# A transformer block on one Trainium2 core: attention in visits of one token tile and four units, and the first FFN layer of chunk 0 by token tiles

## The chip, the core and the metric

The kernel runs on one core of a Trainium2 chip. The core has five engines that run their own instruction queues in order and meet at semaphores: TensorE (PE: matmuls, and with them the loads of the stationary operand, PEld), VectorE (DVE), ScalarE (ACT), GpSimd (POOL) and SyncE (SP, which here issues the DMAs). The metric is the device time of one launch in microseconds (us); lower is better.

## The reference

One pre-norm transformer block over a sequence of 2048 tokens with 576 features, in bf16. The attention has 32 heads of 18 features and works in four segments of 512 tokens: inside a segment it is causal softmax attention, and what lies in earlier segments enters through a compressed memory. The FFN has 4608 hidden features.

```python
# per segment s, per head; phi(t) = t+1 where t>0, exp(t) elsewhere; g = sigmoid(beta)
a_dot = softmax(qs @ ks.T / sqrt(18) + causal_mask) @ vs
a_mem = (phi(qs) @ M) / (phi(qs) @ z + 1e-6)
o     = g * a_mem + (1 - g) * a_dot
M, z  = M + phi(ks).T @ vs, z + phi(ks).sum(tokens)
# the block
h   = x + concat(o) @ wo          # q, k, v come from layernorm(x) @ wq, wk, wv
out = h + gelu_tanh(layernorm(h) @ w1 + b1) @ w2 + b2
```

## The kernel before

The 2048 tokens are cut into eight chunks of 256, a chunk into two token tiles of 128. A segment is two chunks, an even and an odd one. Seven generators ("streams") each produce the work of one stage for all chunks in turn:

- `stream_P(tl)`, one for each token tile of a chunk: load x, layernorm (DVE, with a power on POOL), transpose, the projections to q, k and v (four groups of five matmuls of 432 columns, L294 and L295), transposes of q and k into `QT` and `KT`, and phi of k for the memory. For the first two chunks transposes are matmuls (L320, L401), later they are DMA transposes.
- `stream_M`: the memory `MZacc` and its gated form `MZ_blk`.
- `stream_A`: the attention. A *unit* is four heads (one group g), one tile of 128 queries and one tile of 128 keys. A *visit* is up to 512 score columns for each of the four heads: the scores (L482) are four matmuls at a time, one in each 32-row group of the array, into the four banks `st`; ACT takes the exponential of all of it into one of three buffers `pt` (L488); POOL zeroes what lies above the diagonal (L492), one instruction for each unit on the diagonal; PE multiplies with v (L507), accumulating in the bank `ox`. `st` is there once, so the next visit's scores wait for the exponential. Before the change a visit is one group g with both query tiles: key tiles 0 and 1 together, then 2 and 3 in an odd chunk. Since units above the diagonal are left out, a visit holds 3 units (384 columns) or 4 (512 columns). There are 8 visits in an even chunk and 16 in an odd one, 96 in all; 320 units. After two groups `finish` divides by the softmax's sum and adds the memory's part (L547 to L563). Attention of chunk c begins when P is done for both its token tiles.
- `stream_B(tl)`: the output projection with `wo`, the residual, the second layernorm and its transposition into `xn2T`. It begins when the attention of the whole chunk is done.
- `stream_F1`: the first FFN layer, 36 tiles of 128 hidden features, each five matmuls of 256 columns (L294, L295), evicted two tiles at a time by DVE (L703); then GELU on ACT in pieces of 18 tiles (L711). w1 is streamed from memory; for chunk 0 there are five buffers of four tiles each. It begins when both halves of B are done.
- `stream_F2`: the second FFN layer, four accumulations of 36 matmuls of 288 columns for each chunk (L737).

Every engine's order is fixed while the program is built. The streams hand operations to a planner (`op`, `begin`, `step`): each operation carries an engine, an assumed duration, what it reads and writes, and a due time (now plus an entry of the table `SLACK`). The planner steps through an assumed time; an engine that is free takes the ready operation that is due first, and PE takes the first stream in a list of preferences that can go on. Sorted by the planned start, the operations are then issued. Where PE has nothing to do before the first FFN matmul, the planner puts in *filler* matmuls on the tile `pq` that compute nothing used (L775). ACT has to load a table when it changes between exponential and GELU.

The instructions thus stand in a planned order, but the chip waits on real semaphores: an engine whose next instruction isn't ready stands still, whatever lies behind it.

Of the kernel before, what the change touches and what calls it, by code (L numbers as in the profile page):

```python
# [16 lines left out]
def kernel(  # L17
# [40 lines left out]
    def sbuf(name, shape, dt=BF16):  # L58
# [10 lines left out]
    SLACK = dict(lnp=5, lnb=6.5, pow=4, apply=-8, ek_k=4, relu_k=9, min_k=0.5, add_k=10, mz=2.5, exp=-5, ek=9.5,  # L69
                 relu=13.5, min=4.5, add=0, hb=27, gelu=17.5, finish=3.5, mem=-2, sum=-2, out=8, hd=17, xp=0.5, xb=10,  # L70
                 t_x=34, t_q=19.5, t_k=34, t_o=23, t_h=14, w1=1.5, w2=16, hc=25.5, evict=0, qk=-3, ot=-7, mask=0,
                 lead=1.5, balance=21)
    ops = []
    now, dma_free, table = 0.0, 0.0, "exp"
    free_at = {"PE": 0.0, "SP": 0.0, "ACT": 0.0, "DVE": 0.0, "POOL": 0.0}
    queue = {e: [] for e in free_at}
    writer, readers = {}, {}

    class Op:
        start, end, n = None, NEVER, None  # L80
# [132 lines left out]
    bank_slots.free.append("ox")  # L213
    f_slots = bank_slots
# [82 lines left out]
    def layernorm(who, src, skey, dst, dkey, f32, slack):  # L297
# [6 lines left out]
        def first():  # L304
# [10 lines left out]
                                           op0=ALU.subtract, op1=ALU.mult), ["st" + who, skey], [dkey], slack=slack + SLACK["apply"])  # L315
# [11 lines left out]
    half_P, half_B, t_phi, gelued, begun_P = set(), set(), set(), set(), set()  # L327
# [12 lines left out]
    def stream_P(tl):  # L340
        who = f"p{tl}"
        for c in range(NCH):
# [78 lines left out]
            op("DVE", 0.25, lambda: nc.vector.tensor_scalar(out=ek[:], in0=ek[:], scalar1=1.0, scalar2=None, op0=ALU.min), (), ["ek"], slack=SLACK["min_k"])  # L421
# [403 lines left out]
```

## Time and profile before

| | |
|---|---|
| three runs | 501.04, 501.07 and 501.58 us; median 501.07 us |
| profiled execution | 498.7 us, of which its span (first to last instruction) is 497.0 us |
| granted TensorE clock, mean | 0.996 |
| busy in the span | PE 480.1, PEld 363.1, ACT 292.2, DVE 283.8, POOL 206.6 us |
| PE instructions | 5525 matmuls |

How to read it: a matmul's record is longer than the distance to the next one, since matmuls overlap in the array. The price of a matmul in a stream is therefore taken from the distance of starts, not from its recorded duration. In rows of the trace by time the columns are: start, us from the first start to the last end, engine, line, operation, operands, shape, count, and in brackets the idle time before it with what ended it.

### The profile page before, as it was taken

Reading aid. Unit: us, or ns where it says so; the run is one execution under the profiler, and the core shown is the slowest. Engines: PE = TensorE matmul, PEld = TensorE weight load, DVE = VectorE, ACT = ScalarE, POOL = GpSimd, SP = SyncE. Lnnn points to the kernel's source line nnn. Section 1 sums busy time; section 2 is a strip of 40 time slices with the busy share of each in tenths; the row PEclk is TensorE's granted clock in tenths of the full one; section 3 lists DMA queues with packets and bytes.
Section 4 is the critical chain, followed back from the end, with each engine's and each line's share of the span. In section 5 each row is a group of like instructions: output and inputs, shape, how many; then the busy total and the mean of one; then the engine's idle time right before and its main releaser. Section 6 shows DMA issues by size and latency. Waiting matters only on the chain.

```text
span 497.0 us, 13329 instructions
## 1 busy us (share of the span) xinstructions
PE 480.1 (97%) x5525; PEld 363.1 (73%) x5525; DVE 283.8 (57%) x696; ACT 292.2 (59%) x221; POOL 206.6 (42%) x291
## 2 busy tenths in 40 slices
PE   8999899798999999999999999999999999999997
PEld 5756578556577877766587787767887878878885
DVE  5868765487577534699456434876734443634411
ACT  3477868953557878657518687666357867122210
POOL 5565541279556331779331423596404242200000
PEclk9999999899999999999999999999999999999999
DMA  8985575549877453958977345777854445765411
GB/s 245 299 281 161 102 164 156 137 58 187 175 169 194 143 169 99 228 106 173 196 199 194 124 153 155 175 113 239 195 172 126 144 138 154 203 206 155 139 37 47
DMA packets 117340, 80.89 MB, mean 163 GB/s; under 512 B 56392, under 2 KB 115232, under 8 KB 117280
## 3 DMA queue, kind: packets, MB, share of 16 engines
q1 hardware_dynamic: 117248, 80.04, 62.3%
q8 instruction: 43, 0.70, 0.6%
q14 instruction: 17, 0.14, 0.1%
q0 software_dynamic: 32, 0.01, 0.1%
HBM read 60.10 MB, written 7.08 MB: 135 GB/s over the span
## 4 chain that ended last, share of the span: by engine, by line
PE 81%; DVE 7%; DMA 6%; ACT 2%; SPq 1%; issue 1%; POOL 0%; DVEq 0%; ACTq 0%
PE bank L294 34%; PE bank L737 23%; PE bank L295 8%; PE ox L507 6%; PE st L482 5%; PE ox L737 2%; DMA w1g<-in_B_w_dram 2%; DMA wqkv<-in_A_wk_dram 1%; DMA xT<-xn 1%; PE ox L294 1%; DVE xn L314 1%; DMA xT<-o_nat 1%; ACT hT L711 1%; DVE stats_p L301 1%; DVE r L550 1%
## 5 line engine op out<-in xcount | busy, mean ns | idle before, releaser
L488 ACT ACTIVATE pt<-st 128x2048 bf16<-128x2048 f32 (+1 forms) x96 | 153.0, 1594 | 99.8 <-PE st L482 98.6
L703 DVE CAST hT<-bank 128x512 bf16<-128x512 f32 x139 | 95.7, 689 | 104.3 <-PE bank L295 103.3
L737 PE MATMUL bank<-w_sb,hT 128*128 128x288 bf16 x1044 | 150.7, 287 | 3.0 <-ACT hT L711 3.0
L294 PE MATMUL bank<-xn2T,w1g 128*128 128x256 bf16 x1032 | 149.1, 272 | 0.4 <-DMA w1g<-in_B_w_dram 0.4
L737 PEld LDWEIGHTS <-hT 128*128 128x128 bf16 x1152 | 109.3, 98 | 31.8 <-ACT hT L711 3.3
L492 POOL TENSOR_SCALAR_AFFINE_SELECT pt<-pt 128x512 bf16<-128x512 bf16 x128 | 80.3, 652 | 97.7 <-ACT pt L488 97.6
L294 PEld LDWEIGHTS <-w1g 128*128 128x128 bf16 x1072 | 99.8, 97 | 20.4 <-issue 5.1
L711 ACT ACTIVATE hT<-hT 128x4608 bf16<-128x4608 bf16 (+1 forms) x22 | 65.9, 2996 | 46.0 <-DVE hT L703 45.9
L295 PE MATMUL bank<-xn2T,w1g 65*128 65x256 bf16 x258 | 70.7, 274 | 0.8 <-DMA w1g<-in_B_w_dram 0.8
L294 PE MATMUL bank<-wqkv,xT 128*128 128x432 bf16 x252 | 56.4, 345 | 2.8 <-DMA xT<-xn 2.6
L294 PEld LDWEIGHTS <-xT 128*128 128x128 bf16 x384 | 34.8, 98 | 27.2 <-DMA xT<-xn 3.0
L507 PEld LDWEIGHTS <-pt 128*128 128x128 bf16 x1280 | 43.9, 96 | 9.6 <-issue 6.0
L507 PE MATMUL ox<-v_aug,pt 128*128 128x19 bf16 x1280 | 47.0, 172 | 0.7 <-DVE o_nat L557 0.3
L523 POOL TENSOR_TENSOR pq<-ek,pq 128x512 bf16<-128x512 bf16 x24 | 27.9, 1163 | 27.2 <-DVE ek L522 27.0
L482 PE MATMUL st<-QT,KT 32*128 32x256 bf16 (+1 forms) x768 | 34.8, 255 | 0.7 <-ACT pt L488 0.6
L563 POOL TENSOR_TENSOR o_nat<-t,t 128x288 bf16<-128x288 f32 x24 | 19.4, 806 | 31.2 <-DVE t L560 31.1
L295 PEld LDWEIGHTS <-w1g 65*128 65x128 bf16 x268 | 26.1, 97 | 4.5 <-DMA w1g<-in_B_w_dram 1.4
L741 DVE TENSOR_TENSOR ot<-bank,hc 128x288 bf16<-128x288 f32 x29 | 13.2, 456 | 24.9 <-PE bank L737 21.3
L482 PEld LDWEIGHTS <-KT 32*128 32x128 bf16 x768 | 11.7, 92 | 18.9 <-issue 17.4
L376 ACT CAST qk_pad<-bank 128x432 bf16<-128x432 f32 x31 | 16.0, 520 | 14.4 <-PE bank L295 14.1
L645 POOL TENSOR_TENSOR h_t<-h_t,b_bc 128x576 f32<-128x576 f32 x16 | 20.5, 1279 | 7.1 <-DVE xn L314 7.1
L294 PE MATMUL bank<-wo_t,xT 128*128 128x288 bf16 x128 | 21.3, 293 | 1.9 <-DMA xT<-o_nat 0.9
(98 smaller groups left out, 476.6 us busy)
## 6 DMA issues: line engine op xcount, KB each, us to landing
w1g<-in_B_w_dram SPq DMA_DIRECT2D x67, 512.0 KB
w_sb<-in_B_w_dram SPq DMA_DIRECT2D x6, 864.0 KB
hd<-h_t SPq DMA_DIRECT2D x16, 288.0 KB
hc<-hd SPq DMA_DIRECT2D x32, 144.0 KB
w1g<-in_B_w_dram SPq DMA_DIRECT2D x67, 64.0 KB
x_b<-in_A_x_dram SPq DMA_DIRECT2D x18, 144.0 KB
hT<-in_B_w_dram SPq DMA_DIRECT2D x5, 512.0 KB
out_dram<-ot SPq DMA_DIRECT2D x16, 144.0 KB
```

What stands on the lines that cost most here:

```text
L294: nc.tensor.matmul(out=out_ap, lhsT=lhsT_of(slice(0, P), k), rhs=rhs_of(slice(0, P), k), start=(k == 0), stop=False)
L295: nc.tensor.matmul(out=out_ap, lhsT=lhsT_of(slice(0, KTAIL), 4), rhs=rhs_of(slice(0, KTAIL), 4), start=False, stop=True)
L482: nc.tensor.matmul(out=st4[:, i, o:o + (2 - lo) * P], lhsT=KTs[(s0 + kt // 2) % 3][rows, g, (kt % 2) * P:(kt % 2 + 1) * P], rhs=QTs[c % 2] ...
L488: op("ACT", 0.18 + 4 * off * 0.00083, lambda: nc.scalar.activation(out=pt[:, :, 0:off], in_=st4[:, :, 0:off], func=ACT.Exp, scale=scale), ...
L492: op("POOL", 0.675, lambda o=o: nc.gpsimd.affine_select(out=pt[:, :, o:o + P], in_=pt[:, :, o:o + P], pattern=[[0, 4], [1, P]], compare_op ...
L507: nc.tensor.matmul(out=oxv[:, g % 2, qt, i, :], lhsT=pts[slot][:, i, blk:blk + P], rhs=v_augs[(2 * s0 + kt) % 6][:, 4 * g + i, :], start=o ...
L523: op("POOL", 1.15, lambda: nc.gpsimd.tensor_tensor(out=pq[:], in0=e_g, in1=pq[:], op=ALU.add), ["ek"], ["pq"], slack=SLACK["add"])
L563: op("POOL", 0.7, lambda: nc.gpsimd.tensor_tensor(out=o_dst, in0=t1v, in1=t2v, op=ALU.add), ["t1", "t2"], ok, slack=SLACK["sum"])
L645: op("POOL", 1.36, lambda: nc.gpsimd.tensor_tensor(out=h_t[:], in0=h_t[:], in1=b2_bc[:], op=ALU.add), ["b2"], [("h", tl)], slack=SLACK["hb"])
L703: op("DVE", 0.684, lambda hT=hT, jp=jp, acc=acc: nc.vector.tensor_copy(out=hT[:, 2 * jp:2 * jp + 2, :], in_=acc), [b], [("hT", c % 2, jp)] ...
L711: op("ACT", (f1 - f0) * Q * 0.00083 + 0.18, lambda hT=hT, f0=f0, f1=f1: nc.scalar.activation(out=hT[:, f0:f1, :], in_=hT[:, f0:f1, :], fun ...
L737: nc.tensor.matmul(out=acc, lhsT=hT[:, q, tl * P:(tl + 1) * P], rhs=w2_sb[:, q, hs], start=(q == 0), stop=(q == NF - 1))
```

## The change

Five things change.

1. **Visits.** A visit is now four units of one token tile qt of the queries: `units` runs over four groups (sixteen heads, one half gh of the heads) and the key tiles that the query tile sees, and is cut into pieces of four. All 80 visits have 512 columns. A score matmul has 128 columns, so a visit is sixteen matmuls in four rounds of four row groups (before: eight matmuls in two rounds). `finish` and the memory's part work on one token tile and sixteen heads, as often as before (32 and 24 times).
2. **Finer dependences.** Attention of a token tile begins when P of that tile is done, and B of a tile begins when the attention of that tile is done. With more than two masked units in a visit, the products with v wait for the masks two units at a time.
3. **F1 of chunk 0.** The first 20 of the 36 hidden tiles (five w1 buffers, `AHEAD` = 5) are done for token tile 0 as soon as B of that tile is done, and later again for token tile 1, in matmuls of 128 columns. The other 16 tiles are done for both together, as before. The first GELU piece of chunk 0 then has 22 tiles and the second 14 (before 18 and 18).
4. **The planner** now also assumes that certain DVE operations and POOL's wait for each other (`port`).
5. **All entries of `SLACK`** are new numbers, so the order moves everywhere.

```diff
-    SLACK = dict(lnp=5, lnb=6.5, pow=4, apply=-8, ek_k=4, relu_k=9, min_k=0.5, add_k=10, mz=2.5, exp=-5, ek=9.5,
+    SLACK = dict(head=0, lnp=5.5, lnb=9.5, pow=-8.5, apply=8, ek_k=23, relu_k=40, min_k=5, add_k=9, mz=5, exp=13.5,
...
+        if getattr(o, "port", False):
+            dur += max(0.0, port_until["POOL" if o.eng == "DVE" else "DVE"] - now)
+            port_until[o.eng] = now + dur
...
-    def scores(c, g, pieces, slot):
+    def scores(c, qt, units, slot):
...
+            for n, (g, kt) in enumerate(units):
                 for i in range(4):
                     rows = slice(32 * i, 32 * i + 32)
+                    nc.tensor.matmul(out=st4[:, i, n * P:(n + 1) * P],
+                                     lhsT=KTs[(c - c % 2 + kt // 2) % 3][rows, g, (kt % 2) * P:(kt % 2 + 1) * P],
+                                     rhs=QTs[c % 2][rows, g, qt * P:(qt + 1) * P], start=True, stop=True, tile_position=(32 * i, 0))
...
+            for qt in range(2):
+                for gh in range(2):
+                    units = [(g, kt) for g in range(4 * gh, 4 * gh + 4) for kt in range(2 * (c % 2) + qt + 1)]
+                    visits += [(c, qt, gh, n == 0, n + 4 == len(units), units[n:n + 4]) for n in range(0, len(units), 4)]
...
+                yield need(lambda: (c, qt) in half_P and (c < 2 or (c - 2, qt) in half_B) and (seg == 0 or 2 * seg - 1 in done_M),
...
+                parts = [(0, 1), (2, 3)] if sum(kt == own for _, kt in units) > 2 else [(0, 1, 2, 3)]
...
-            yield need(lambda: c in done_A, xT_slots, idle=False)
+            yield need(lambda: (c, tl) in half_A, xT_slots, idle=False)
...
-            for jp in range(NF // 2):
+            if c == 0:
+                for tl in range(2):
+                    for n in range(AHEAD):
...
+                        yield need(lambda: (0, tl) in half_B, f_slots, xk[tl:tl + 1] + wk)
...
+                            op("PE", 5 * 0.0565, lambda acc=acc, a=a, wt=wt, tl=tl: mm5(
+                                acc[:, a, :], lambda r, k: wt[r, k, a * P:(a + 1) * P],
+                                lambda r, k: xn2T[0][r, k, tl * P:(tl + 1) * P]), xk[tl:tl + 1] + wk, [b])
...
+            for jp in range(0 if c else 2 * AHEAD, NF // 2):
```

What this does to the queues is seen at three places. The first is PE at the first FFN matmul of the program. `xn2T_88` is the transposed input of the FFN for chunk 0, `w1g_66` the first w1 buffer, `xT_87` the input of a q, k, v projection, `KT_104` the keys of chunk 0, `pt_109` a buffer of exponentials. Before, this place comes after 109 filler matmuls and 16 visits:

```order
L294 MATMUL bank_142<-wqkv,xT_87 128x432
...
L295 MATMUL bank_142<-wqkv,xT_87 128x432
L294 LDWEIGHTS w1g_66
L294 MATMUL bank_141<-xn2T_88,w1g_66 128x256
...
L295 MATMUL bank_141<-xn2T_88,w1g_66 128x256
L482 LDWEIGHTS KT_104
L482 MATMUL st_139<-QT_103,KT_104 128x256
```

After the change it comes after 70 filler matmuls and 10 visits, behind the memory's matmuls (`phik_pad`):

```order
L447 LDWEIGHTS phik_pad_95
L447 MATMUL bank_143<-v_aug_99,phik_pad_95 128x76
L300 LDWEIGHTS w1g_66
L300 MATMUL bank_141<-xn2T_88,w1g_66 128x128
...
L301 MATMUL bank_141<-xn2T_88,w1g_66 128x128
L518 LDWEIGHTS pt_109
L518 MATMUL ox<-v_aug_98,pt_109 128x19
```

The first FFN layer has moved ahead of six visits, in halves of 128 columns. Of the fillers 38 stood ahead of the first projection and 71 behind it; now 42 stand ahead and 28 behind.

The second place is ACT at the first GELU of the program (`hT_122` is the hidden layer of chunk 0, `ek` the exponential of queries for the memory). Before:

```order
L488 ACTIVATE pt_107<-st_139 128x4x384
L711 ACT_TABLE_LOAD
L711 ACTIVATE hT_122<-hT_122 128x4608
L488 ACT_TABLE_LOAD
L488 ACTIVATE pt_108<-st_139 128x2048
L488 ACTIVATE pt_109<-st_139 128x4x384
L711 ACT_TABLE_LOAD
L711 ACTIVATE hT_122<-hT_122 128x4608
```

After:

```order
L495 ACTIVATE pt_108<-st_139 128x2048
L528 ACTIVATE ek<-QT_102 128x512
L741 ACT_TABLE_LOAD
L741 ACTIVATE hT_122<-hT_122 128x5632
L495 ACT_TABLE_LOAD
L495 ACTIVATE pt_109<-st_139 128x2048
L741 ACT_TABLE_LOAD
L741 ACTIVATE hT_122<-hT_122 128x3584
```

The first piece has grown from 18 hidden tiles to 22 (5632 elements), and one exponential instead of two stands between the pieces.

The third place is PE where the second FFN layer begins (`w_sb,hT_122`). Before, sixteen of its matmuls stand in a row, then a product with v and a visit, and then the matmuls on tiles 16 to 19:

```order
L295 MATMUL bank_143<-xn2T_88,hT_123 128x256
L737 LDWEIGHTS hT_122
L737 MATMUL bank_141<-w_sb,hT_122 128x288
...
L507 LDWEIGHTS pt_109
L507 MATMUL ox<-v_aug_98,pt_109 128x19
...
L482 LDWEIGHTS KT_106
L482 MATMUL st_139<-QT_102,KT_106 128x256
```

After, sixteen stand in a row, then the output projection of chunk 1 (`wo_t`) and a visit:

```order
L301 MATMUL bank_141<-xn2T_88,hT_123 128x256
L767 LDWEIGHTS hT_122
L767 MATMUL bank_143<-w_sb,hT_122 128x288
...
L300 LDWEIGHTS xT_87
L300 MATMUL bank_142<-wo_t,xT_87 128x288
...
L489 LDWEIGHTS KT_106
L489 MATMUL st_139<-QT_102,KT_106 128x128
```

Ahead of it now stand all of the sixteen hidden tiles of chunk 0 that are done for both token tiles, with a single visit among them; behind it, tiles 16 to 19 follow after ten `wo` matmuls and one visit, and tiles 20 to 23 after a product with v, a memory product and five projection matmuls.

More of the change, by code (lines that the diff above doesn't have):

```diff
@@ L495, in scores @@
-        return placed
-    def weighted(c, g, placed, slot):
+        op("PE", 0.43, go, score_keys(c, qt, units), sk)
+        op("ACT", 1.88, lambda: nc.scalar.activation(out=pt[:], in_=st4[:], func=ACT.Exp, scale=scale), sk,
+           [("pt", slot, n) for n in range(4)], slack=SLACK["exp"], table="exp")
+        for n, (g, kt) in enumerate(units):
+            if kt == own:
+                op("POOL", 0.65, lambda n=n: nc.gpsimd.affine_select(
+                    out=pt[:, :, n * P:(n + 1) * P], in_=pt[:, :, n * P:(n + 1) * P], pattern=[[0, 4], [1, P]],
+                    compare_op=ALU.is_ge, fill=0.0, base=0, channel_multiplier=-1), (), [("pt", slot, n)], slack=SLACK["mask"])
@@ L501, in go @@
         def go():
-            opens = g % 2 == 0 and placed[0][0] == 0
-            for kt, lo, o in placed:
+            opens = first
+            for n in part:
+                g, kt = units[n]
                 for i in range(4):
-                    for qt in range(lo, 2):
-                        blk = o + (qt - lo) * P
-                        nc.tensor.matmul(out=oxv[:, g % 2, qt, i, :], lhsT=pts[slot][:, i, blk:blk + P],
-                                         rhs=v_augs[(2 * s0 + kt) % 6][:, 4 * g + i, :], start=opens, stop=False,
-                                         skip_group_check=True)
-                        opens = False
@@ L512, in weighted @@
-        n = sum(4 * (2 - lo) for _, lo, _ in placed)
-        op("PE", n * 0.025, go, [("pt", slot)] + vk, ["ox"])
-    def memory_in(c, g):
-        q2 = QTs[c % 2][:, g:g + 2, :]
-        qk = [("QT", c % 2, 0), ("QT", c % 2, 1)]
-        e_g = ek[:].rearrange("p h d -> p (h d)")[:, 0:2 * Q].rearrange("p (u q) -> p u q", u=2)
-        op("ACT", 0.63, lambda: nc.scalar.activation(out=e_g, in_=q2, func=ACT.Exp), qk, ["ek"], slack=SLACK["ek"], table="exp")
-        op("POOL", 0.61, lambda: nc.gpsimd.tensor_scalar(out=pq[:], in0=q2, scalar1=BIG, scalar2=0.0, op0=ALU.min, op1=ALU.max),
+                    nc.tensor.matmul(out=oxv[:, 4 * (g % 4) + i, :], lhsT=pts[slot][:, i, n * P:(n + 1) * P],
+                                     rhs=v_augs[(2 * s0 + kt) % 6][:, 4 * g + i, :], start=opens, stop=False, skip_group_check=True)
@@ new lines, in go, with memory_in @@
+                    opens = False
+        op("PE", len(part) * 0.1, go, [("pt", slot, n) for n in part] + value_keys(c, units), ["ox"])
+    def memory_in(c, qt, gh):
+        q4 = QTs[c % 2][:, 4 * gh:4 * gh + 4, qt * P:(qt + 1) * P]
+        qk = [("QT", c % 2, qt)]
+        e_g = ek[:].rearrange("p h d -> p (h d)")[:, 0:4 * P].rearrange("p (g q) -> p g q", g=4)
+        op("ACT", 0.63, lambda: nc.scalar.activation(out=e_g, in_=q4, func=ACT.Exp), qk, ["ek"], slack=SLACK["ek"], table="exp")
+        op("POOL", 0.62, lambda: nc.gpsimd.tensor_scalar(out=pq[:], in0=q4, scalar1=BIG, scalar2=0.0, op0=ALU.min, op1=ALU.max),
```

203 lines of the change are left out of this document (103 added, 100 removed).

## The prediction

> **What bounds the kernel now.** I read the page's busy times first, then the chain that ended last, then the busy times either side of the first FFN matmul (at 63.75 us), then who made PE wait behind it.
>
> ```profile
> span 497.0 us, 13329 instructions
> PE 480.1 (97%) x5525; PEld 363.1 (73%) x5525; DVE 283.8 (57%) x696; ACT 292.2 (59%) x221; POOL 206.6 (42%) x291
> PE 81%; DVE 7%; DMA 6%; ACT 2%; SPq 1%; issue 1%; POOL 0%; DVEq 0%; ACTq 0%
> 0.00:63.75 63.75, 58.16 (x709) 38.59 (x710) 45.23 (x130) 40.07 (x44) 36.65 (x62) 1.00 0.77 219
> 63.75:497.00 433.25, 421.99 (x4817) 324.56 (x4815) 238.60 (x567) 252.09 (x178) 169.95 (x230) 0.99 0.61 155
> PE bank L737 <- ACT hT L711: 3.0, 1, 3.0
> PE bank L294 <- DMA xT<-xn: 2.6, 1, 2.6
> PE bank L294 <- DMA xT<-o_nat: 0.9, 1, 0.9
> ```
>
> PE is the bound: 97% busy, 81% of the chain, and behind 63.75 us it stands still for 11 of 433 us. Two waits make half of that: one of 3.0 us for a GELU, one of 2.6 us for a DMA transpose. So only two things shorten the kernel: less PE work, and less time in which PE does nothing useful. The second is larger than it looks, because the filler on `pq` counts as busy. Its share, in the two stretches 0 to 8.6 and 8.6 to 63.75 us (columns: PE, PEld, clock, DMA):
>
> ```profile
> 0.00:8.60 8.60, 5.92 (x37) 4.27 (x37) 1.00 0.76 207
> 8.60:63.75 55.15, 9.65 (x72) 6.44 (x72) 1.00 0.78 220
> ```
>
> In the first stretch the data haven't arrived. In the second, 72 records cover up to 9.65 us in which no stream had work for PE.
>
> **Visits.** Distances of starts on PE price them. The rows show a visit of four units, its second round alone, a visit of three units, and a run of products with v.
>
> ```profile
> 301.88 0.27 PE L295 MATMUL bank<-xn2T,w1g 65*128 65x256 bf16 x1
> 302.08 0.40 PE L482 MATMUL st<-QT,KT 32*128 32x256 bf16 x8
> 302.41 0.61 PE L294 MATMUL bank<-xn2T,w1g 128*128 128x256 bf16 x4
> 302.20 0.28 PE L482 MATMUL st<-QT,KT 32*128 32x256 bf16 x4
> 299.42 0.27 PE L295 MATMUL bank<-xn2T,w1g 65*128 65x256 bf16 x1
> 299.63 0.34 PE L482 MATMUL st<-QT,KT 32*128 32x256 bf16 x8
> 299.91 0.56 PE L507 MATMUL ox<-v_aug,pt 128*128 128x19 bf16 x16
> 303.46 0.45 PE L507 MATMUL ox<-v_aug,pt 128*128 128x19 bf16 x12
> 303.76 0.41 PE L737 MATMUL bank<-w_sb,hT 128*128 128x288 bf16 x2
> 65.29 0.60 PE L294 MATMUL bank<-xn2T,w1g 128*128 128x256 bf16 x4
> 65.72 0.27 PE L295 MATMUL bank<-xn2T,w1g 65*128 65x256 bf16 x1
> 65.84 0.33 PE L507 MATMUL ox<-v_aug,pt 128*128 128x19 bf16 x7
> 14.61 0.61 PE L401 MATMUL ox<-ident,qk_pad 128*128 128x128 bf16 x8
> 15.06 0.61 PE L401 MATMUL bank<-ident,qk_pad 128*128 128x128 bf16 x8
> ```
>
> Five matmuls of 256 columns take 65.84 − 65.29 = 0.55 us, 0.11 us each. So the visit of four units costs 302.41 − 301.88 − 0.11 = 0.42 us: 0.09 before the first round (302.08 − 301.99), 0.12 for it (302.20 − 302.08, against 0.11 for its columns) and 0.21 for the second with the way out. The visit of three units costs 299.91 − 299.42 − 0.11 = 0.38 us. There are 32 and 64 of them:
>
> ```profile
> L488 ACT ACTIVATE pt<-st 128x1536 bf16<-128x1536 f32 x64 | 92.9, 1452 | 55.6 <-PE st L482 55.3
> L488 ACT ACTIVATE pt<-st 128x2048 bf16<-128x2048 f32 x32 | 60.1, 1877 | 44.2 <-PE st L482 43.3 <-POOL pt L492 0.7
> L492 POOL TENSOR_SCALAR_AFFINE_SELECT pt<-pt 128x512 bf16<-128x512 bf16 x128 | 80.3, 652 | 97.7 <-ACT pt L488 97.6
> ```
>
> That is 32 × 0.42 + 64 × 0.38 = 37.8 us of PE. After, there are 80 visits of four rounds of 128 columns, which the trace doesn't show. A full-array matmul of 128 columns takes (15.06 − 14.61)/8 = 0.056 us. With 0.01 us more for a round, as in the round above, a visit is 0.09 + 3 × 0.066 + (0.21 − 0.053) = 0.45 us, and 80 make 36.0: **−1.8 us**. Below, a round pays for its columns alone and the visit stays at 0.42: 33.6, −4.2 us. Above, a round of 128 columns lasts as long as one of 256, 0.12 us: 0.09 + 3 × 0.12 + 0.157 = 0.61, 48.6 us, +10.8 us. I take the middle one, because it differs least from the round that the trace shows.
>
> On ACT, 80 × 1.88 = 150.4 us stands against 153.0, worth nothing while PE is the bound. Masks are as many as before (128 × 0.65 us), but up to four now lie in one visit: 2.6 us between exponential and product. PE needs other work meanwhile; behind the first FFN matmul it has some, before it the fillers.
>
> **F1 of chunk 0 in halves.** 20 hidden tiles for 256 tokens, 20 × 0.55 = 11.0 us, become 40 × 5 × 0.056 = 11.2 us: **+0.2 us**. The ten evictions keep their 512 columns.
>
> **The fillers.** The order has 28 of them behind the first projection instead of 71. The price of one:
>
> ```profile
> 18.23 1.80 PE L775 MATMUL bank<-pq 128*128 128x256 bf16 x15
> 19.97 0.34 PE L482 MATMUL st<-QT,KT 32*128 32x256 bf16 x8
> 55.11 0.35 PE L482 MATMUL st<-QT,KT 32*128 32x256 bf16 x8 [0.61 <-ACT pt L488]
> ```
>
> (19.97 − 18.23)/15 = 0.116 us, and 43 fewer are 5.0 us. What fills their place is the FFN of token tile 0 (20 × 5 × 0.056 = 5.6 us), drawn ahead of six visits, and an attention that starts on the first token tile alone. The four more ahead of the first projection cost nothing: they stand where PE waits for data. But a filler that goes may leave a bare wait. The third row shows one: where no filler stood, scores waited 0.61 us for the previous exponential. In the new order eight visits still follow one another between the second and the first FFN matmul. I let a third of that row, 0.2 us, return at each of them, 1.6 us in all, an estimate between 0 and 5.0. **Net −3.4 us.**
>
> **The GELU wait.** PE stands 3.0 us before a second-layer matmul; ACT's rows around it:
>
> ```profile
> 90.86 1.28 ACT L711 ACT_TABLE_LOAD   x1
> 92.15 4.04 ACT L711 ACTIVATE hT<-hT 128x4608 bf16<-128x4608 bf16 x1
> 96.25 1.54 PE L737 MATMUL bank<-w_sb,hT 128*128 128x288 bf16 x7 [3.03 <-ACT hT L711]
> ```
>
> The second piece came at 96.2, when PE had passed the 18 hidden tiles of the first. In the new order the first piece has 22 tiles: 1.28 + 4.04 × 22/18 = 6.2 us with its table. It can start when hidden tiles 20 and 21 are evicted; from there PE still has 14 tiles (7.7 us), a visit and a product with v (0.45 + 16 × 0.025), less about 0.7 us of eviction: 7.9 us. So F2 finds its input. ACT then needs 1.28 + 1.88 + 1.28 + 4.04 × 14/18 = 7.6 us to the end of the second piece, at 13.8 us on this count. PE comes to tile 20 after 16 + 4 second-layer matmuls (0.12 us each, 2.4), ten `wo` matmuls (1.2), a visit, a product, the memory and five projections (0.45 + 0.40 + 0.14 + 0.92), at 13.4. About 0.3 us of wait is left: **−2.7 us**. If one more exponential gets between, the 3.0 us stay.
>
> Finer dependences, `port` and the new `SLACK` issue no instruction of their own; what they move is in the terms above, or in waits that I can't count. The 2.6 us wait for the transposed `xn` may go or come anywhere; I leave it.
>
> **Sum.** −1.8 + 0.2 − 3.4 − 2.7 = −7.7 us. The profiled execution took 498.7 us (1.7 around its span), so 491.0; the median of the runs is 2.4 us above it: 501.07 − 7.7 = **493.4 us**.
>
> **Rivals.** *The idle time stays and only changes its name* (chance 0.25). The attention chain at the start is paced by ACT, not PE: an exponential of 1.88 us, the way back to PE and the next scores, with projections' casts between. Then fillers become waits, and the GELU wait stays. For it speaks that ACT is 40 of 63.75 us busy there, and the 0.61 us row; against it that PE has 5.6 us more of real work in reach, and that 20 exponentials replace 24 in chunks 0 and 1. The sum is −1.8 + 0.2: 499.5 us.
>
> *Weight loads set the round* (0.13). Each round needs four new weight loads. If they hide behind 256 columns but not behind 128, the round stays at 0.12 us, and the sum is +10.8 + 0.2 − 3.4 − 2.7 = +4.9: 506.0 us, **slower**. The turning point: the other terms save 5.9 us, so visits may cost 43.7, 0.55 each, a round of (0.55 − 0.09 − 0.157)/3 = 0.10 us. For it speaks that the 0.12 us can't be told apart from a load of that length hidden behind the columns. Against it: the products with v load 128 by 128 weights for every matmul and start (303.76 − 303.46)/12 = 0.025 us apart. The Trainium skill, "TensorE: Matmul & The Clock Gate", section "LDWEIGHTS (loading the stationary operand)", has a load last P/1.2 ns by its columns alone, 107 ns for 128 columns whatever the rows; by that rule the round would be this rival's. The 0.025 us rows contradict it for full-height loads; of 32-row loads under 128 columns no run here shows anything.
>
> The forecast has 0.62. **Range:** at its low end no exponential wait returns (−1.6), visits pay for columns only (−2.4), and the `xn` wait goes (−2.6): 486.8. At its high end stands the first rival, with one more wait of 2 us: 501.5. Left out is the slower rival, with some tail. A measurement of this kernel can tell about 0.2%, 1.0 us, from no change. **Chances:** faster 0.78 (forecast 0.62, 0.16 of the first rival), same 0.07 (first rival), slower 0.15 (0.13 and 0.02).
>
> **What would show it.** The first FFN matmul stands six visits earlier; ahead of it they took (63.75 − 19.97)/15 = 2.9 us each, so it stands near 46 us instead of 63.75. Visits: sixteen score matmuls and 0.45 us from the end of the work before to the start of the work behind; 0.55 or more proves the slower rival. Filler between the first projection and the first FFN matmul takes 3.3 us, and bare waits there don't grow by more than 1.6 us. The wait of L767 for GELU is below 0.5 us. The forecast is wrong if waits of PE behind the first FFN matmul exceed before's, as would be with masks on POOL or `xn` transposes late in the even chunks, where two visits with four masks each follow one another.

## The result, and the profile after

The changed kernel takes 483.74 us (median of four runs, 480.94 to 484.0) beside 501.32 us for the kernel before (four runs, 501.04 to 502.31): a ratio of 0.9633, 95% interval 0.9595 to 0.9671. That is 17.6 us less; 7.7 were forecast, and the time lies below the range of 486.8 to 501.5 us. The profiled execution took 483.72 us with a span of 481.9, against 498.7 and 497.0: 15.0 us less from profile to profile. The working below explains these 15.0; the other 2.6 are taken up under experiment e8.

The page's first lines after the change, and its chain that ended last:

```profile
span 481.9 us, 14443 instructions
PE 471.6 (98%) x6098; PEld 369.1 (77%) x6098; DVE 283.4 (59%) x688; ACT 290.0 (60%) x205; POOL 206.8 (43%) x291
PE 88%; DMA 7%; DVE 2%; SPq 1%; ACT 1%; POOL 0%; issue 0%; ACTq 0%; DVEq 0%; POOLq 0%
```

PE is still the bound, and more so: 88% of the chain instead of 81%. DVE has gone from 7% to 2%. The busy times of the other engines have hardly moved, so nothing was won there.

The busy times behind the first FFN matmul, which now stands at 45.42 us instead of 63.75 (columns: PE, PEld, DVE, ACT, POOL, clock, DMA share, GB/s); then the same stretches for the filler's line alone (PE, PEld, clock, DMA share, GB/s):

```profile
7.90:45.42 37.52, 35.33 (x544) 24.61 (x543) 29.18 (x74) 26.74 (x30) 21.97 (x33) 1.00 0.82 248
45.42:481.94 436.52, 429.73 (x5514) 339.48 (x5510) 248.47 (x589) 261.32 (x175) 177.94 (x239) 1.00 0.65 161
```

```profile
0.00:7.90 7.90, 6.30 (x42) 4.79 (x42) 1.00 0.72 191
7.90:45.42 37.52, 4.57 (x30) 2.49 (x28) 1.00 0.82 248
```

Behind the first FFN matmul PE stands still for 6.8 us instead of 11.3. Between the first projection and that matmul the filler's busy time fell from 9.65 to 4.57 us, as forecast (5.0 less). The waits of PE behind the first FFN matmul (total, times, longest):

```profile
PE bank L300 <- DMA xT<-xn: 2.1, 1, 2.1
PE bank L300 <- DMA xT<-o_nat: 1.3, 2, 0.9
```

The wait for GELU is gone, and the wait for `xn` is left, shorter by half a microsecond. The waits between the first projection and the first FFN matmul, the longest of the kernel before and then of the changed one:

```profile
PE bank L320 <- DVE xn L314: 0.8, 2, 0.6
PE st L482 <- ACT pt L488: 0.6, 1, 0.6
PE bank L320 <- DVE o_nat L557: 0.6, 1, 0.6
PE bank L294 <- ACT xT L616: 0.5, 1, 0.5
PE bank L294 <- DVE h_t L628: 0.5, 1, 0.5
```

```profile
PE st L489 <- ACT pt L495: 0.7, 2, 0.4
PE ox L300 <- DMA wqkv<-in_A_wk_dram: 0.7, 1, 0.7
PE bank L300 <- DMA wqkv<-in_A_wv_dram: 0.4, 1, 0.4
```

Scores wait for the exponential as long as before (0.7 and 0.6 us). Gone are the waits on the way out of the attention: for the divided output (`o_nat`), for its transposed copy (`xT`) and for the residual (`h_t`).

The middle of the program, PE by time (start, duration, line, operands, shape, count, and the idle time ahead with its releaser; between the last two rows shown, a product with v and four memory matmuls are left out):

```profile
84.61 2.12 PE L767 MATMUL bank<-w_sb,hT 128*128 128x288 bf16 x16
87.63 0.66 PE L300 MATMUL bank<-wo_t,xT 128*128 128x288 bf16 x4 [0.90 <-DMA xT<-o_nat]
88.13 0.29 PE L301 MATMUL bank<-wo_t,xT 65*128 65x288 bf16 x1
88.35 0.40 PE L489 MATMUL st<-QT,KT 32*128 32x128 bf16 x16
88.69 0.67 PE L300 MATMUL bank<-wo_t,xT 128*128 128x288 bf16 x4
89.19 0.29 PE L301 MATMUL bank<-wo_t,xT 65*128 65x288 bf16 x1
89.32 0.65 PE L767 MATMUL bank<-w_sb,hT 128*128 128x288 bf16 x4
92.61 1.02 PE L300 MATMUL bank<-wqkv,xT 128*128 128x432 bf16 x4 [2.09 <-DMA xT<-xn]
```

A matmul of 288 columns takes 89.32 − 89.19 = 0.13 us here, so the visit costs 88.69 − 88.13 − 0.13 = 0.43 us with all its sixteen matmuls, what a visit of 512 columns cost in eight (0.42). The weight loads don't set the rounds, though each lasts longer than a round:

```profile
L489 PEld LDWEIGHTS <-KT 32*128 32x128 bf16 x1280 | 18.6, 92 | 14.7 <-issue 12.9
```

A load of the scores' weights is recorded with 92 ns, but 1280 of them (117.8 us one by one) cover only 18.6 us together: they overlap.

Where PE once stood 3.0 us before a second-layer matmul, the second layer goes on at 89.32 with no wait; PE waits 0.9 us for `o_nat` ahead of it.

**Where 15.0 us went.** Useful work, filler and waits can be separated by the distances of starts on PE. Each shape has a usual distance to the next start (in us: 0.109 for 256 columns, 0.122 for 288, 0.182 for 432, 0.056 for 128, 0.025 for a product with v; a visit 0.428, or 0.374 with 384 columns). What a distance has above the usual one is a wait if it is over 0.12 us, and a small loss otherwise; a filler has the usual distance of its 256 columns. Summed over each trace (us):

| | before | after | difference | forecast |
|---|---|---|---|---|
| visits, at the usual distance | 37.6 | 34.2 | −3.4 | −1.8 |
| all other work | 421.1 | 421.6 | +0.5 | +0.2 |
| filler behind the first projection (72 and 28) | 7.9 | 3.1 | −4.8 | −5.0 |
| waits from there to 60 us | 5.0 | 3.2 | −1.8 | +1.6 |
| filler and waits ahead of the first projection | 7.0 | 6.5 | −0.5 | 0 |
| waits behind 60 us: for GELU | 3.2 | 0 | −3.2 | −2.7 |
| the other waits behind 60 us | 6.5 | 5.4 | −1.1 | 0 |
| small losses | 3.9 | 3.3 | −0.6 | 0 |
| first matmul's start, and the end | 4.8 | 4.8 | 0 | 0 |
| span | 497.0 | 481.9 | −15.0 | −7.7 |

(The rows are rounded, so their sums can be 0.2 off. Each profile has one stretch of 3.4 us at half clock, told of under e8; what it costs is among the small losses before, and mostly among the other waits after.)

### The profile page after: what moved, and what is told of

Read it like the earlier page. It is cut to its first block, busy times and chain, and to the rows that moved or that the text cites. A ratio compares the mean times of both kernels' runs of the same rounds, so it can differ in the third digit from the quotient of the medians.

```text
span 481.9 us, 14443 instructions
## 1 busy us (share of the span) xinstructions
PE 471.6 (98%) x6098; PEld 369.1 (77%) x6098; DVE 283.4 (59%) x688; ACT 290.0 (60%) x205; POOL 206.8 (43%) x291
## 4 chain that ended last, share of the span: by engine, by line
PE 88%; DMA 7%; DVE 2%; SPq 1%; ACT 1%; POOL 0%; issue 0%; ACTq 0%; DVEq 0%; POOLq 0%
PE bank L300 36%; PE bank L767 26%; PE bank L301 9%; PE ox L518 6%; PE st L489 5%; DMA xT<-xn 2%; DMA x_p<-in_A_x_dram 2%; PE ox L767 2%; DMA wqkv<-in_A_wv_dram 2%; PE ox L300 1%; DMA w1g<-in_B_b_dram 1%; ACT pt L495 1%; PE bank L447 1%; PE bank L541 1%; PE bank L805 1%; DMA xT<-o_nat 1%
## 5 line engine op out<-in xcount | busy, mean ns | idle before, releaser
L495 ACT ACTIVATE pt<-st 128x2048 bf16<-128x2048 f32 x80 | 150.2, 1878 | 61.9 <-PE st L489 61.6
L767 PE MATMUL bank<-w_sb,hT 128*128 128x288 bf16 x1080 | 155.7, 286 | 0.0
L300 PE MATMUL bank<-xn2T,w1g 128*128 128x256 bf16 (+1 forms) x1040 | 146.3, 269 | 0.0
L733 DVE CAST hT<-bank 128x512 bf16<-128x512 f32 x126 | 86.7, 690 | 86.9 <-PE bank L301 85.8
L741 ACT ACTIVATE hT<-hT 128x4608 bf16<-128x4608 bf16 (+3 forms) x22 | 65.9, 2996 | 67.1 <-DVE hT L733 67.0
L301 PE MATMUL bank<-xn2T,w1g 65*128 65x256 bf16 (+1 forms) x260 | 70.4, 271 | 0.1
L518 PE MATMUL ox<-v_aug,pt 128*128 128x19 bf16 x1280 | 45.8, 172 | 0.1
L489 PE MATMUL st<-QT,KT 32*128 32x128 bf16 x1280 | 32.2, 217 | 0.7 <-ACT pt L495 0.7
L489 PEld LDWEIGHTS <-KT 32*128 32x128 bf16 x1280 | 18.6, 92 | 14.7 <-issue 12.9
L317 POOL TENSOR_TENSOR rstd_b<-rstd_b,mhalf 128x1 f32<-128x1 f32 x16 | 8.8, 552 | 44.6 <-DVE rstd_b L312 44.6
L637 DVE TENSOR_TENSOR h_t<-bank,x_b 128x288 f32<-128x288 f32 x32 | 14.6, 457 | 13.5 <-PE bank L301 13.1
```

Of the source, the lines that this page charges most:

```text
L300: nc.tensor.matmul(out=out_ap, lhsT=lhsT_of(slice(0, P), k), rhs=rhs_of(slice(0, P), k), start=(k == 0), stop=False)
L301: nc.tensor.matmul(out=out_ap, lhsT=lhsT_of(slice(0, KTAIL), 4), rhs=rhs_of(slice(0, KTAIL), 4), start=False, stop=True)
L489: nc.tensor.matmul(out=st4[:, i, n * P:(n + 1) * P], lhsT=KTs[(c - c % 2 + kt // 2) % 3][rows, g, (kt % 2) * P:(kt % 2 + 1) * P], rhs=QTs[ ...
L495: op("ACT", 1.88, lambda: nc.scalar.activation(out=pt[:], in_=st4[:], func=ACT.Exp, scale=scale), sk, [("pt", slot, n) for n in range(4)], ...
L518: nc.tensor.matmul(out=oxv[:, 4 * (g % 4) + i, :], lhsT=pts[slot][:, i, n * P:(n + 1) * P], rhs=v_augs[(2 * s0 + kt) % 6][:, 4 * g + i, :] ...
L733: op("DVE", 0.684, lambda hT=hT, jp=jp, acc=acc: nc.vector.tensor_copy(out=hT[:, 2 * jp:2 * jp + 2, :], in_=acc), [b], [("hT", c % 2, jp)] ...
```

## The experiments

Two theories stood at the start. One: the terms of the forecast are right in kind, and the change won more because its finer gates let PE find work where I had expected waits. The rival: the gain is not the structure's at all but lies in the new order (`SLACK` and `port`), or in a state of the clock. All runs stand in one table; "before" was timed beside each. Filler (all of it) and waits are from each run's trace by the account above; the kernel before has 13.5, 6.4 and 9.7 us there, the change 9.3, 3.4 and 5.4.

| | median, us (runs) | ratio to before, 95% | first FFN matmul | filler | waits ahead of 60 us | behind |
|---|---|---|---|---|---|---|
| e1 F1 of chunk 0 whole | 485.55 (4) | 0.9708, 0.9670 to 0.9746 | 64.2 | 13.2 | 4.0 | 4.2 |
| e2 coarse gates | 493.51 (4) | 0.9868, 0.9827 to 0.9909 | 57.3 | 10.4 | 4.2 | 13.2 |
| e3 two waits filled | 484.96 (6) | 0.9701, 0.9661 to 0.9741 | 46.1 | 12.7 | 3.6 | 3.2 |
| e4 before, rounds split | 496.31 (8) | 0.9926, 0.9898 to 0.9955 | 64.1 | 13.9 | 6.3 | 6.4 |
| e5 visits alone | 494.79 (4) | 0.9897, 0.9866 to 0.9927 | 62.3 | 10.6 | 6.1 | 11.3 |
| e6 old table | 499.19 (10) | 0.9965, 0.9933 to 0.9997 | 40.9 | 7.6 | 5.1 | 20.1 |
| e7 no port | 490.37 (4) | 0.9805, 0.9772 to 0.9837 | 47.4 | 12.5 | 3.1 | 7.8 |
| e8 before, waits filled | 495.45 (6) | 0.9902, 0.9879 to 0.9925 | 64.4 | 20.0 | 6.1 | 1.4 |
| e9 before, new order | 499.14 (10) | 0.9972, 0.9948 to 0.9996 | 64.5 | 15.3 | 4.9 | 10.5 |
| e10 visits, own order | 491.20 (4) | 0.9816, 0.9790 to 0.9842 | 63.3 | 14.0 | 4.6 | 7.6 |
| e11 the change again | 482.69 (6) | 0.9659, 0.9630 to 0.9688 | 45.8 | 10.5 | 2.6 | 3.1 |
| e12 one wait filled | 483.90 (5) | 0.9681, 0.9655 to 0.9706 | 45.6 | 12.2 | 2.8 | 4.0 |

### e1: the first FFN layer of chunk 0 whole again

```diff
-    LATER, AHEAD = 0, 5
+    LATER, AHEAD = 0, 0
```

> The changed kernel with the first FFN layer of chunk 0 done for both token tiles together (AHEAD = 0), all else as changed, replanned. Theory A (the 7 us less of lost PE time before the first 60 us come from the FFN of token tile 0, which gives PE real work there): most of it comes back, +4 to +6 us against the changed kernel (483.7), fillers behind the first projection rise from 28 to 59. Theory B (they come from the attention that starts on one token tile alone): at most +2 us.

Measured: 485.55 us. Its busy times behind 60 us (columns as above), and its two longest waits there:

```profile
60.00:500.00 440.00, 417.69 (x5214) 331.03 (x5212) 240.85 (x562) 248.66 (x165) 168.38 (x226) 1.00 0.61 152
```

```profile
PE bank L300 <- DVE hT L733: 1.1, 1, 1.1
PE bank L767 <- ACT hT L741: 0.6, 1, 0.6
```

The first FFN matmul is back at 64.2 us and the filler at 13.2, but most of the gain stays. The halves are worth the difference of the ratios, 0.9708 − 0.9633 or 0.9659: 2 to 4 us, with intervals of 2 us either side, so the run falls between the two theories. The halves bring 3 to 4 us less filler, and the GELU wait's last 0.6 us is gone with them. (With `AHEAD` = 0 the GELU pieces of chunk 0 are 18 and 18 tiles again, here and in e5 and e10.)

### e2: coarse gates

```diff
-                yield need(lambda: (c, qt) in half_P and (c < 2 or (c - 2, qt) in half_B) and (seg == 0 or 2 * seg - 1 in done_M),
+                yield need(lambda: c in done_P and (c < 2 or c - 2 in done_B) and (seg == 0 or 2 * seg - 1 in done_M),
...
-            yield need(lambda: (c, tl) in half_A, xT_slots, idle=False)
+            yield need(lambda: c in done_A, xT_slots, idle=False)
```

(The start of the attention stream waits for both token tiles of chunk 0 in the same way.)

> The changed kernel with the old, coarse gates: attention of a chunk waits for P of both token tiles, B of a tile waits for the attention of the whole chunk; visits of four units and the FFN of chunk 0 by token tiles stay. Theory A (the FFN by halves carries the gain): +1 to +3 us against the changed kernel. Theory B (the finer gates carry it): +5 us or more.

Measured: 493.51 us, 10 us above the change. Its busy times behind 60 us, and its longest waits there:

```profile
60.00:500.00 440.00, 419.33 (x5311) 331.21 (x5309) 244.43 (x568) 253.25 (x167) 172.80 (x230) 0.99 0.65 154
```

```profile
PE bank L767 <- ACT hT L741: 2.3, 1, 2.3
PE bank L300 <- DMA w1g<-in_B_w_dram: 1.8, 2, 1.1
PE bank L300 <- DMA xT<-o_nat: 1.7, 3, 1.0
```

From 60 us to the end of the span (492.8) are 432.8 us, of which PE is busy for 419.3: 13.5 us of standing, 2.3 of it for GELU again, where the change has 421.94 − 415.15 = 6.8 and e1 has 424.14 − 417.69 = 6.4. The filler is only 1 us above the change's. So the gates don't act where I had looked, on the filler ahead of the first FFN matmul, but on waits all over the program. How much of it is the gate and how much an order that was made for other gates, this run alone doesn't tell; e10 takes it up.

### e3 and e12: the waits of the changed kernel filled

Useless matmuls stand where PE waits for `xn` (and in e3, for `o_nat` too).

```diff
+    def warm(acc, n):
+        for _ in range(n):
+            nc.tensor.matmul(out=acc[:, 0:256], lhsT=ident[:], rhs=wqkv[:, 0, 0:256], start=True, stop=True)
...
+                fill = 19 if (c, tl, ch) == (3, 0, 0) else 0
...
+                fill = 8 if (c, tl, hf) == (1, 1, 0) else 0
```

e12 has the same edit with `fill = 0` in the second place.

> The changed kernel with 8 and 19 matmuls of no use put on PE just ahead of its two waits for DMA transposes (0.9 us at 87 us, 2.1 us at 90 us); the order is else the same. Theory C (PE's clock is halved for 3.4 us after a wait of 2 to 3 us, and that costs the difference between the run at clock 1.0, 480.9, and those at 0.996, 483.7): every run is at clock 1.0 and at about 481. Rival (the clock has another cause, or the waits alone cost the time): no change, 483.7.

> The changed kernel with 19 matmuls of no use ahead of the projection that waits 2.1 us for transposed xn. Theory C (a wait of that length halves the clock for 3.4 us at a cost of 1.7 to 2.8 us): clock 1.0 and 1.7 to 2.8 us less than the changed kernel beside it. Rival (the clock costs nothing here, since what follows waits for data anyway, or the fillers delay as much as they save): within 1 us of it.

Measured: 484.96 and 483.90 us, against 482.69 for the change timed beside e12. The place in e12, PE by time, and the longest wait of its trace behind 60 us:

```profile
90.65 2.23 PE L305 MATMUL bank<-wqkv,ident 128*128 128x256 bf16 x19
92.72 0.89 PE L300 MATMUL bank<-wqkv,xT 128*128 128x432 bf16 x4
```

```profile
PE bank L300 <- DMA xT<-o_nat: 2.7, 3, 1.0
```

The wait is covered. All five runs of e12 and five of the six of e3 had a mean clock of 0.999 or 1.0; one of e3 had 0.996 and took 487.85 us. Without any fill, six of the ten runs of the change have 0.999 or 1.0, so this shows little of the clock. And nothing was won: in e12 `o_nat` waits of 2.7 us stand where the change repeated (e11) has 1.1. This is no better version than the change itself.

### e4: the kernel before, with rounds of 128 columns

The 256-column score matmuls are cut in two; everything else is as before.

```diff
-                    nc.tensor.matmul(out=st4[:, i, o:o + (2 - lo) * P],
+                    nc.tensor.matmul(out=st4[:, i, o:o + P],
...
-                                     rhs=QTs[c % 2][rows, g, lo * P:Q], start=True, stop=True, tile_position=(32 * i, 0))
+                                     rhs=QTs[c % 2][rows, g, lo * P:(lo + 1) * P], start=True, stop=True, tile_position=(32 * i, 0))
+                for i in range(4 if lo == 0 else 0):
...
+                    nc.tensor.matmul(out=st4[:, i, o + P:o + 2 * P],
```

> The kernel before with every score matmul of 256 columns cut into two of 128, so that visits keep their number and contents and get three or four rounds instead of two. Theory of the trace after (a round costs its columns and some 6 ns, the fixed cost is the visit's): within 1 us of the kernel before. Rival (weight loads set a round): 128 rounds more at 0.06 to 0.12 us, +7.7 to +15 us.

Measured: 496.31 us, 4.5 us faster than before, where 1 us either way was expected. The visit of three units that the prediction priced, now in three rounds:

```profile
302.62 0.27 PE L295 MATMUL bank<-xn2T,w1g 65*128 65x256 bf16 x1
302.82 0.23 PE L482 MATMUL st<-QT,KT 32*128 32x128 bf16 x4
302.89 0.22 PE L487 MATMUL st<-QT,KT 32*128 32x128 bf16 x4
302.95 0.22 PE L482 MATMUL st<-QT,KT 32*128 32x128 bf16 x4
303.10 0.57 PE L512 MATMUL ox<-v_aug,pt 128*128 128x19 bf16 x16
```

Rounds of 128 columns start 0.07 and 0.06 us apart, and the visit costs 303.10 − 302.62 − 0.11 = 0.37 us, against 0.38 in two rounds. The median over all visits is 0.431 us for four rounds and 0.375 for three (0.426 and 0.373 before). So the number of rounds costs nothing: the rival in which weight loads set the round is refuted, its 0.12 us were half as long. Why this kernel is faster than before is not told by its visits. In its trace the waits for `xn` and w1 are shorter (the account has 1.5 for `xn` against 2.9, and none for w1 behind 60 us against 1.8); what shortened these two DMA waits stays open. So two programs with the same planned order can differ by some 4 us for a reason that these runs don't show; steps of that size between the kernels below are to be read with this in mind.

### e5: visits alone

The edits of e1 and e2 together, with the change's own numbers in `SLACK`.

> The changed kernel with coarse gates and with the first FFN layer of chunk 0 whole: of the structure, only the visits of four units are left, with the new table and port. Theory B (gates carry the gain): about as with coarse gates alone, 493 to 496. Theory D (visits carry it, 80 of 0.43 us instead of 96): 490 or less.

Measured: 494.79 us. Visits save 3.4 us and the filler is 2.9 less; the waits stay (6.1 and 11.3 us against 6.4 and 9.7, a GELU wait of 3.3 us among them). Its numbers in `SLACK` were made for another structure.

### e6 and e7: the change with the old numbers, and without port

```diff
-    SLACK = dict(head=0, lnp=5.5, lnb=9.5, pow=-8.5, apply=8, ek_k=23, relu_k=40, min_k=5, add_k=9, mz=5, exp=13.5,
+    SLACK = dict(head=0, lnp=5, lnb=6.5, pow=4, apply=-8, ek_k=4, relu_k=9, min_k=0.5, add_k=10, mz=2.5, exp=-5, ek=9.5,
...
```

```diff
-        if getattr(o, "port", False):
+        if False:
```

> The changed kernel, structure and port as changed, with the numbers of SLACK of the kernel before (head = 0). Theory B (structure: gates and visits): at most +4 us against the changed kernel (483.7). Theory E (the new table is what removes waits of PE; the structure alone does little): +8 us or more, with waits for GELU and DMA transposes behind 60 us as long as before's 9.7.

> The changed kernel with a planner that does not count waits between DVE and POOL (port off), table and structure as changed. If the port in the plan matters on the chip: +3 us or more, in waits of PE for DVE or POOL. If it only shifts the plan: within 2 us. The order has 57 fillers behind the first projection instead of 28, so up to +3.4 us in fillers by themselves.

Measured: 499.19 us for e6, 490.37 for e7. Behind 60 us in e6, busy times and the longest waits:

```profile
60.00:500.00 440.00, 420.00 (x5280) 331.23 (x5276) 243.97 (x568) 251.12 (x167) 169.54 (x230) 0.99 0.62 152
```

```profile
PE bank L300 <- DVE hT L733: 3.7, 4, 1.5
PE bank L300 <- DMA xT<-xn: 2.4, 2, 2.0
PE bank L300 <- DMA w1g<-in_B_w_dram: 2.0, 2, 1.6
PE bank L767 <- ACT hT L741: 2.0, 1, 2.0
```

e6 reaches its first FFN matmul at 40.9 us, earlier than the change, with only 7.6 us of filler, and gives it all back: PE stands 438.0 − 420.0 = 18.0 us behind 60 us. The longest new wait is PE's for DVE's evictions of the hidden layer (L733). In e7 the order falls apart less: 2.0 us for GELU and 2.6 for `o_nat`.

```profile
PE bank L300 <- DMA xT<-o_nat: 2.6, 3, 1.4
PE bank L767 <- ACT hT L741: 2.0, 1, 2.0
```

So with the old numbers, which I had priced at nothing, 16 of the 17 us are lost, and without the assumption on DVE and POOL about 7, *in this structure*. That is the rival's half of the truth; e9 tests the other half.

### e8: the kernel before with its two long waits filled

31 useless matmuls stand where PE waited for GELU and 24 where it waited for `xn`; no work is left out.

```diff
+                fill = 24 if (c, tl, ch) == (4, 0, 0) else 0
...
+                                for _ in range(fill if q == 18 else 0):
+                                    nc.tensor.matmul(out=side, lhsT=ident[:], rhs=wqkv[:, 0, 0:224], start=False, stop=False,
```

> The kernel before with 31 matmuls of 224 columns put ahead of the matmul that waits 3.0 us for GELU, and 24 of 256 ahead of the projection that waits 2.6 us for transposed xn. Theory C (a long wait halves the clock for 3.4 us, 1.7 us each time, and this makes before's runs range from 497 to 504): clock 1.0 in all runs, 497 to 498.5. Rival: the clock falls elsewhere as well, and the median stays at 500 to 501.

Measured: 495.45 us, 5.2 us faster, less even than the 497 to 498.5 of theory C, though the fill itself does no useful work. Kernel before around its GELU wait and just behind it, then e8 at the same place (busy times of PE, PEld, DVE, ACT, POOL, then the granted clock):

```profile
92.90:96.30 3.40, 0.37 (x3) 0.07 (x3) 3.15 (x12) 3.38 (x2) 0.56 (x2) 1.00 0.26 53
96.60:100.00 3.40, 3.40 (x17) 2.14 (x16) 0.25 (x1) 2.86 (x3) 1.21 (x3) 0.50 0.44 86
```

```profile
93.00:96.40 3.40, 3.40 (x47) 3.17 (x44) 3.03 (x11) 3.40 (x1) 0.93 (x2) 1.00 0.26 53
96.40:100.00 3.60, 3.54 (x31) 2.66 (x29) 1.32 (x6) 3.57 (x4) 0.91 (x2) 1.00 0.47 91
```

Behind the wait the kernel before has a stretch of 3.41 us at half clock (17 matmuls in 3.4 us where e8 does 31 in 3.6): 1.7 us of lost work. All six runs of e8 have a mean clock of 0.999 or 1.0. The 47 runs of the kernel before in these experiments fall into groups by their clock: nine at 0.999 to 1.0 with a median of 498.56 us, 23 at 0.996 to 0.997 with 500.16, ten at 0.992 to 0.993 with 501.47, five lower with 504.41. Each half-clock stretch, 0.0035 of the mean clock, thus goes with 1.3 to 1.6 us more; a run with one more stretch may also have a longer wait ahead of it, which these groups don't tell apart. At like clock the change is worth 498.56 − 481.8 = 16.8 us (of the ten runs of the change, e11's among them, six are at 0.999 or 1.0, with a median of 481.8) or 500.16 − 483.9 = 16.3 (the other four, at 0.996). So the clock gives under 1 us of the 17.6. The rest of the step from 15.0 is that the profiled execution of the kernel before, 498.7 us at a clock of 0.996, lay below all 23 others with that clock (499.3 to 501.9).

Of e8's 5.2 us the clock explains 500.69 − 498.56 = 2.1. The rest are waits that its edit doesn't touch: those for w1 and `o_nat` behind 60 us (1.8 and 1.2 us in the account of before) are not in its trace. Why they went is not settled; as in e4, it is some 3 us that the edit gives no reason for.

### e9 and e10: an order of its own for the old structure, and for the new visits alone

Both have the `port` assumption and numbers for `SLACK` that were searched for that structure: e9 for the kernel before, e10 for e5's (shown is e9's edit without the new numbers).

```diff
-    SLACK = dict(lnp=5, lnb=6.5, pow=4, apply=-8, ek_k=4, relu_k=9, min_k=0.5, add_k=10, mz=2.5, exp=-5, ek=9.5,
...
+        if getattr(o, "port", False):
+            dur += max(0.0, port_until["POOL" if o.eng == "DVE" else "DVE"] - now)
+            port_until[o.eng] = now + dur
```

> The kernel before in structure (visits of one group, coarse gates, FFN of chunk 0 whole), with the changed kernel's port in the planner and SLACK numbers that I searched for this structure by the length of the plan. Theory E (an order that fits, port and table, is the gain, whatever the structure): 490 or less. Theory S (the structure lets PE be fed, an order alone doesn't): 495 to 501, with fillers before 60 us not below 14.

> The kernel with visits of four units, coarse gates and the FFN of chunk 0 whole (as in the run of the visits alone, 494.8), with port, and SLACK searched for this structure. If the gates carry the gain: 492 or more. If visits and an order that fits carry it, and the coarse gates only suffered from a table made for fine ones: 486 to 489.

Measured: 499.14 us for e9 and 491.20 for e10, beside 500.16 for the kernel before. The largest wait of e9 behind 60 us and its largest ahead of that, then the largest of e10 behind 60 us:

```profile
PE bank L739 <- ACT hT L713: 3.0, 1, 3.0
PE st L484 <- ACT pt L490: 1.1, 2, 0.6
```

```profile
PE bank L297 <- DMA w1g<-in_B_w_dram: 3.1, 4, 1.6
```

A new order alone brings the old structure 1.0 us. The rival that the whole gain is the order's falls with that, as far as one search can show it: another search might find a better one. With the new visits a new order brings 9.0 us; that lies between the 486 to 489 us of one theory and the 492 of the other and decides for neither. The steps from before to the change, each with an order of its own (e1 with the change's), are then: visits and order −9.0 us (e10), finer gates from 0.9816 to 0.9708, −5.4 us, F1 in halves −2 to −4 us. This is a way of sharing out the gain and no proof of each share: how good each search was isn't known, and e4 and e8 have 3 to 4 us without a reason.

### e11: the change again

> The changed kernel once more, on the same chip as the run beside it: 481 to 484, at a clock of 0.996 to 1.0.

Unchanged and beside e9, e10 and e12: 482.69 us, ratio 0.9659, 0.9630 to 0.9688, the first result again. Its profiled execution had a mean clock of 1.000 and a span of 479.5 us, and its longest wait is another one:

```profile
PE bank L300 <- DMA xT<-o_nat: 1.1, 2, 0.9
```

The 2.1 us wait for `xn` is not a property of the order: in this execution it doesn't occur. The second GELU piece of chunk 0 and the second layer's tiles 20 to 23 behind it:

```profile
87.67 3.19 ACT L741 ACTIVATE hT<-hT 128x3584 bf16<-128x3584 bf16 x1
91.69 0.65 PE L767 MATMUL bank<-w_sb,hT 128*128 128x288 bf16 x4
```

The piece ends at 90.86 us, and PE comes to its first tile, tile 22, at 91.69 + 2 × 0.12 = 91.93, 1.07 us later. PE had stood still for 0.92 us (the row above) between tiles 15 and 16.

## Why the prediction was wrong

The direction was right, and so were the sizes for the fillers, F1 and GELU. Three terms erred on the same side: the waits ahead of the first FFN matmul by 3.4 us, the waits that the order sets by some 2.2, the visits by 1.6. From profile to profile −7.7 us was forecast and −15.0 measured. The range's low end, 6.6 us lower still, was −14.3 from profile to profile, so the profiled execution alone lies only 0.7 us beyond it. The rest of the 3.1 us below the range comes from the step to the medians: I took the 2.4 us between before's profiled execution and its median as the change's too, but before's profiled execution was an unusually fast one (e8) and the change's (483.72) was not.

- **The step that failed most** reads "I let a third of that row, 0.2 us, return at each of them, 1.6 us in all". None returned. The wait for the exponential is 0.85 us in the account of both traces, and the waits of that stretch fell by 1.8 us in all: a difference of 3.4, the largest. What fell is the way from the attention through B, for `o_nat`, `xT` and `h_t`: 1.46, 0.58 and 0.64 us in the account of before, 0.14 after, while waits for the weights `wqkv` grew from 0.3 to 1.4. I had looked only at the wait that a missing filler uncovers, and not at those that stood bare already. It would be natural to lay their end to the token tile that starts by itself, but the runs don't show that: the three waits are missing in e9 too, in the old structure with another order. Waits ahead of 60 us are 6.4 us before, 4.9 in e9, 6.1 with the visits alone (e5), 4.6 with visits and an order of their own (e10), 4.2 with coarse gates (e2), 4.0 with F1 whole (e1), and 3.4 and 2.6 with everything. So a new order alone takes them away; what the structure adds to it stays open. The price of the fillers (−5.0) was right (−4.8).
- **Visits.** "With 0.01 us more for a round" was too much: a round of 128 columns takes 0.06 us, and a visit 0.431 us, not 0.45: −3.4 us, not −1.8. The row nearest to it was the right one; the supplement that I took over from the 256-column round does not hold for all four rounds. (The sum itself, 0.445, was rounded up to 0.45: 0.4 us over 80 visits.) The rival went wrong at the step from a load's length to the round's: the loads' records last 92 ns with 32 rows and 96 with 128, but they overlap. The Trainium skill, "TensorE: Matmul & The Clock Gate", section "LDWEIGHTS (loading the stationary operand)", gives a load of 128 columns the same time, 107 ns, whatever its rows. The records come near to that, and neither the 0.06 us between rounds nor the 0.025 us that the prediction held against it contradicts it: both are distances between starts.
- **"Finer dependences, `port` and the new `SLACK` issue no instruction of their own"** is true, and putting them at nothing was wrong. They set which waits occur, those of the first point among them: 1.7 us of other waits and small losses behind 60 us in the profile, 0.5 ahead of the first projection, and with the old numbers (e6) nearly the whole gain is lost. A change of a planner's table has a price that isn't in any row, and my range had one wait of 2.6 us for it.
- **GELU.** The size was right, −3.2 against −2.7, but the reason given, the larger first piece, is neither enough nor needed. With the piece of 22 tiles and another order, or coarse gates, the wait is back (e2, e6, e7: 2.3, 2.0 and 2.0 us); with pieces of 18 it is 3.3 us in e5, 0.6 in e1 and none in e10. It goes by the order, by where that puts the second layer against the two pieces. There was luck in it, too: under e11 0.92 of the 1.07 us by which PE came late enough were spent in a wait for `o_nat` that the forecast did not have.
- **F1 in halves.** Its price (+0.2) was right to 0.3 us. Its benefit, less filler, was counted as part of the fillers' term; e1 shows 2 to 4 us for the whole of it.
- **Rivals.** "The idle time stays and only changes its name" is what e6 shows: first FFN matmul at 40.9 us, 20.1 us of waits behind 60 us, no gain. With the numbers of the change it doesn't happen. "Weight loads set the round" is refuted by the 0.431 us in the change and in e4.
- **Checks that I had named.** First FFN matmul near 46 us: 45.42. Visit 0.45 us: 0.43. Filler behind the first projection 3.3 us: 3.1 by distances (4.57 by records, whose ends overlap other work). GELU wait below 0.5 us: none.

Shown are the price of a visit, the fall of the fillers and of the waits by the account, and that structure with the old numbers (e6) and one new order on the old structure (e9) each give little, and both together much. That the gates bring some 5 us by fewer waits is argued from e10 and e1, whose orders differ too. Open are which part of the order ends which wait, why e4 and part of e8 are faster than before through waits that their edits don't touch, and how much a longer search would give the old structure.

## What to carry to other kernels

Where every engine's order is fixed in advance, price a structural change together with an order made for it: the structure with the old table (e6) and a new table made for the old structure (e9) were each worth 1 to 2 us here, and structure and table together 17. Count useful PE time from distances of starts, since useless matmuls count as busy; and where a filler goes, ask which engine the waits beside it name before letting them come back.

## What the hardware showed beyond that

A wait of PE can be followed by a stretch of 3.41 us at half clock, but its length alone doesn't tell. Before, PE does 0.37 us of work between 92.90 and 96.30 us, and the clock is 0.50 from 96.62. After, it waits 2.1 us up to 92.61, and the clock is 0.50 from 93.27 (columns as above, the clock ahead of the DMA share). But behind the 2.6 us for `xn` in the kernel before (122.6 to 125.2 us) the clock stays at 1.00, as the second row shows:

```profile
93.30:96.70 3.40, 3.40 (x13) 1.66 (x11) 0.86 (x2) 0.52 (x1) 3.10 (x3) 0.50 0.25 48
125.20:128.70 3.50, 3.50 (x40) 2.18 (x41) 1.07 (x5) 2.37 (x4) 0.61 (x1) 1.00 0.78 233
```

The traces' records of the clock tell them apart. In each trace the clock changes only on a grid of steps of 3.413 us: before, it is at full clock from 4.46 us and at half from 96.62, 27 steps on. What goes with the half clock is how long PE stands still inside one step. The GELU wait lies whole, 3.0 us, in the step that ends at 96.62; the wait for `xn` is cut by the grid line at 123.93 into two pieces of 1.3 us. In the fourteen traces PE stands still for 1.4 to 3.0 us in each of the eleven steps ahead of a half-clock stretch; every step above 1.77 us was followed by one, and between 1.36 and 1.77 some were and some were not.

The Trainium skill, "TensorE: Matmul & The Clock Gate", section "What's actually happening", has the half clock follow one idle window of about 3.4 us. The step and the length of the stretch agree; but in no case here was such a window idle as a whole.

Useless matmuls in the waits kept the clock at 0.999 or above in all six runs of e8, where nine of 47 runs of the same kernel without them have that. For the changed kernel e3 and e12 show no such difference.
